# First queries' second layer moved into the second half of a mixture-of-experts loop, with operands made ahead for the last part

## The chip, the cores and the metric

One Trainium2 chip, one core of it. The metric is the device time of one launch in microseconds. The engines named below: PE (TensorE, matrix multiply), ACT (ScalarE), DVE (VectorE), POOL (GpSimd) and SP (SyncE); SP and POOL also issue the transfers (DMA), each from a queue of its own that is worked through in order.

## The reference, cut to what matters

```python
def _A_ref(x, wqkv, wo):                      # S=2048, D=512, H=32, Dh=16
    q, k, v = ...(x @ wqkv)
    phi = lambda t: jnp.where(t > 0, t + 1, jnp.exp(t)) + 1e-6
    pq, pk = phi(q), phi(k)
    kv = einsum("bhsd,bhse->bhde", pk, v)
    z  = einsum("bhsd->bhd", pk)
    o  = (pq . kv) / (pq . z + 1e-6)
    return o @ wo

def _B_ref(x, w_gate, w1, w2):                # E=8, F=1792, K=8: every expert is used
    gates = softmax(x @ w_gate)
    for e in range(E):
        out = out + gates[:, e] * (silu(x @ w1[e]) @ w2[e])

g = sigmoid((x * gate_w).sum(-1))
return g * _A_ref(x, wqkv, wo) + (1 - g) * _B_ref(x, w_gate, w1, w2)
```

All values are float32.

## The kernel before

The output has two addends that share one loop. An expert is two matrix products with `silu` between them. The attention half is put into the same form: its "first layer" is the query projection with `phi` in place of `silu`, its "second layer" is a matrix that the kernel makes from `kv` and `wo` (`wpd`, four tiles written in `fold`). So the loop treats the queries as a ninth expert of smaller width.

Every operand is split into a high and a low part (`act_copy` rounds to the high part on ACT, a `tensor_sub` on DVE gives the low part), and `mm3` (L57 to L60) multiplies in three passes. The block products use seven instead of eight multiplications, in a fixed order of products `ORDER = P1, P7, P2, P4, P6, P5, P3`, with sums and differences of blocks made on DVE (`prep` for weights, `differ` for hidden values).

The tokens are handled in two halves, h = 0 and 1. A *part* is one expert (or the queries, e == E) on one half. An expert's part has 7 *groups* (pairs of 128 hidden features) and 49 *ticks* of second layer; a query part has 2 groups and 14 ticks. The loop runs over steps `u`. Seven steps make the first layer of one group (`up`), each step one product on PE of 6 matmuls of 128x512; the same step does one tick of second layer (`tick`, again 6 matmuls) for an earlier part. The second layer is `LAG` = 58 steps behind. The order of the work on every engine is written out by hand: what `up`, `other` and `mid` emit is the order in each engine's queue.

Groups run in the order: queries of half 0, the eight experts of half 0, queries of half 1, the eight experts of half 1 (`m.groups`, L109 to L113; `m.G1` is where half 1 begins). Second layers run in the order of `m.parts`: eight experts of half 0, eight of half 1, and then both query parts, 28 ticks at the end. Since the queries of half 1 put 14 steps of first layer between the halves, the second half runs at `LAG1` = 72 steps behind, and `clock` (L526) leaves 14 steps at the joint without a tick. After the last group, at step 812, steps hold a tick alone.

What lies around the change:

- `load` (L147) brings the raw weights of a group, from SP. Where `with_second(part)` holds, it also brings the second-layer weights, and `prep` splits those and writes them to DRAM (`stash`, seven transfers of 256 KB for a group, from two buffers of tag `ws`). This holds for the experts of half 0 and for the queries of half 1, whose two groups carry `wpd`.
- `load_w2` (L688) brings one 512 KB tile of stashed second-layer weights for every two ticks, from SP, into three buffers.
- `x_next` (L626) brings the split input blocks of half 1 in steps G1-1 and G1: 14 tiles of 512 KB, from SP.
- `hidden` (L553) applies `silu` on ACT, or `phi` (two passes on ACT, one on DVE) and a store to `pqd`.
- `evict` (L717) and `finish` (L708) take a finished product out of PE's banks: for an expert, a multiplication by its gate (`wb`) on DVE and an accumulating DMA into `acct` from POOL; for the queries, an addition to `sums`, tiles that `load_sums` (L898) has read back.
- `queries_load`, `queries_first`, `queries_last` divide the queries by the normaliser, 20 steps for each of four blocks, in the first four parts of half 1. `load_query` (L891) reads the results back from POOL.
- `rows` (L919) turns `sums` on PE and writes the output.
- `gates` (L811) makes softmax and sigmoid of the gate logits after step 11. `normaliser` and `gate_rows` follow.
- `keys`, before the loop, makes `phi(k)`, the gate logits and `kv`. Its first products wait for the first loads and splits.

Of the kernel before, what the change touches and what calls it, by code (L numbers as in the profile page):

```python
# [42 lines left out]
def gated_mix_kernel(ctx: ExitStack, tc: tile.TileContext, xT, x, wk, wv, wqkv_q, wo, wm, out):  # L43
# [58 lines left out]
    m.parts = [SimpleNamespace(e=e, h=h, n=NPAIR) for h in range(2) for e in range(E)]  # L102
    m.parts += [SimpleNamespace(e=E, h=h, n=2) for h in range(2)]
# [4 lines left out]

    m.groups = []  # L109
    for i in (2 * E, *range(E), 2 * E + 1, *range(E, 2 * E)):  # L110
        part = m.parts[i]
# [3 lines left out]
    m.G1 = m.parts[2 * E + 1].g0  # L115
# [15 lines left out]
def weights(m):  # L131
# [12 lines left out]
    def with_second(part):  # L144
        return (part.e == E) == (part.h == 1)

    def load(g):  # L147
        if g >= m.NG:
            return
        part, q = m.groups[g]  # L150
        both = with_second(part)
        if g >= m.G1 + 4:
# [12 lines left out]
        if both:  # L165
            for i in range(2):
                src = m.wm[part.e * NPAIR + q][:, i, D:] if part.e < E else m.wpd[2 * q + i]
                nc.sync.dma_start(r[:, :, i, 1, :], src.rearrange("p (h f) -> p h f", h=2))
# [4 lines left out]
    def o_tile(name, tag, bufs, width):  # L173
        return w1p.tile([P, 2, width], F32R, name=name, tag=tag, bufs=bufs)

    def prep(g, step):
# [21 lines left out]
        def stash(prod, src):  # L200
            i = part.e * 7 * NPAIR + m.ORDER.index(prod) * part.n + q
            nc.sync.dma_start(m.w2stash[i // 2][:, i % 2].rearrange("p (c f) -> p c f", c=2), f32(src))

# [4 lines left out]
        def low2(n, src, *prods):  # L208
            if both:
                w = ws.pop((g, n))  # L210
                v.tensor_sub(two(w, 1), src, f32(two(w, 0)))  # L211
                for half, prod in enumerate(prods):
                    stash(prod, w[:, :, half * HALF:(half + 1) * HALF])
# [15 lines left out]
        elif step == 2:  # L229
            o = ops[g][6][0]  # L230
            v.tensor_sub(o[:, 1], r[:, 1, 1, 0], f32(o[:, 0]))
            if both:
                w = ws.pop((g, 0))
                v.tensor_sub(w[:, 1, :HALF], r[:, 0, 0, 1], f32(w[:, 0, :HALF]))
                stash("P1", w[:, :, :HALF])
# [19 lines left out]
    m.raw_tile, m.load, m.prep = raw_tile, load, prep  # L255
# [3 lines left out]
def keys(m):  # L259
# [46 lines left out]
    sp = sf_tile("sp")[:NH, :].rearrange("p (c f) -> p c f", c=KT)  # L306
# [22 lines left out]


# [45 lines left out]
    band(sp, [[P, KT], [1, P]], -DH)  # L376
    spread = sf_tile("spread", F32R)
    for i in range(2):
        act_copy(spread[i * NH:(i + 1) * NH], sp.rearrange("p c f -> p (c f)"))
    nc.gpsimd.memset(f32(spread)[2 * NH:], 0.0)  # L380
    nc.gpsimd.dma_start(m.spd, f32(spread))
# [9 lines left out]
    def g_done(t, g, ps):  # L391
        if g == 0:
# [4 lines left out]
            pk[t] = sf_tile(f"pk{t}"), h  # L397
# [50 lines left out]

    banks = [up_bank(f"g0_{t}")[:, :G[0]] for t in range(NTT)]
# [60 lines left out]
def experts(m, misc):  # L510
# [5 lines left out]
    NE = 2 * E  # L516
# [4 lines left out]
    LAG1 = LAG + 14  # L521
    T1 = E * PT
    U1 = LAG + T1
    part_of = [part for part in m.parts for _ in range(7 * part.n)]

    def clock(u):  # L526
        return u - (LAG if u < U1 else LAG1)


    def mine(n, u):  # L530
        return 0 <= n < T1 if u < U1 else T1 <= n < NTICK
# [111 lines left out]

    def differ(u):
# [3 lines left out]
        for pairs, offs in ((NPAIR, (None, 6, 15, 29)), (2, (-3, -1, 1, 5))):  # L648
            for kind, off in enumerate(offs):
                if off is None or not mine(clock(u) - off, u):  # L650
                    continue
                n = clock(u) - off
                part, prod, q = place(n)
                if part.n != pairs or prod != "P1":
                    continue
                t11, t12, t21, t22 = blocks(part, q)
                if kind == 0:
                    v.tensor_sub(t12, t22, t12)
                elif kind == 1:
                    v.tensor_add(t11, t11, t12)  # L660
                elif kind == 2:
                    v.tensor_sub(t21, t21, t11)
                else:
                    v.tensor_sub(t11, t22, t11)
# [3 lines left out]
    def high(n):  # L668
        part, prod, q = place(n)
        s = blocks(part, q)[SRC[prod]]  # L670
        if n % 6 == 5:
            h = m.xpool.tile([P, 2, TB], F32R, name=f"ho{n}", tag="xs", bufs=2)
# [11 lines left out]
    NW = T1 // 2  # L684

    ENDS = (NU + 12 - LAG1) // 2

    def load_w2(i):  # L688
        at, tag, bufs = (m.w1p, "o", 4) if i > ENDS and i % 2 else (m.w2p, "w2", 3)
        w2s[i] = at.tile([P, 2, 2, HALF], F32R, name=f"w2{i}", tag=tag, bufs=bufs)  # L690
        j = i % NW if i < 2 * NW else NW + (i - 2 * NW) % 7
# [10 lines left out]
    def load_wb(i):  # L702
        e, h = m.parts[i].e, m.parts[i].h
        wb[e, h] = m.xpool.tile([P, 2, TB], F32, name=f"wb{i}", tag="xs", bufs=2)
# [12 lines left out]
    def evict(part, prod, sub):  # L717
        b = pb[BANK[prod], sub]
        e = f"{part.h}_{part.e}{sub}"
        if part.e == E:  # L720
# [90 lines left out]
    def gates():  # L811
        g, wgt, gat, mx = m.lg[:, :, :E], m.wgt, m.gat, m.mx
        v.tensor_reduce(mx, g, axis=AX.X, op=ALU.max)
        v.tensor_sub(g, g, mx[:, :, None].to_broadcast([P, NT, E]))
        nc.scalar.activation(wgt, g, AF.Exp)
        nc.scalar.activation(gat, m.lg[:, :, E], AF.Exp, scale=-1.0)
        v.tensor_scalar(gat, gat, 1.0, None, op0=ALU.add)
        v.reciprocal(gat, gat)
        v.tensor_reduce(mx, wgt, axis=AX.X, op=ALU.add)
        v.reciprocal(mx, mx)  # L820
        v.tensor_mul(wgt, wgt, mx[:, :, None].to_broadcast([P, NT, E]))
        v.tensor_scalar(mx, gat, -1.0, 1.0, op0=ALU.mult, op1=ALU.add)
        v.tensor_mul(wgt, wgt, mx[:, :, None].to_broadcast([P, NT, E]))
# [15 lines left out]
    Q = SimpleNamespace(az=None)  # L839

    def queries_load(i):
        if Q.az is None:
            Q.az = m.raw_tile("az", F32R)
# [47 lines left out]
    def load_query(h, i):  # L891
        q, f, t = i // 4, i // 2 % 2, i % 2
        part = m.parts[NE + h]
        d = raw[part.g0 + q, f, t] = r_tile(f"q{h}{i}")
        nc.gpsimd.dma_start(d, m.pqd[h, t, 2 * q + f])


    def load_sums(h, j):  # L898
        for dt in range(KT):
            if dt % 2 == 0:  # L900
                r = m.xpool.tile([P, 2, TB], F32, name=f"tl{h}{j}{dt}", tag="x", bufs=14)
            sums[h, dt, j] = r[:, dt % 2]
            nc.gpsimd.dma_start(r[:, dt % 2], m.acct[h, j, dt])
# [7 lines left out]
    def rows_out(ps, h, i):  # L911
        r = r_tile(f"o{h}{i}")
# [6 lines left out]
    def rows(h, i):  # L919
        ps = ps_tile(f"o{h}{i}", "a")  # L920
        turn(ps, h, i, range(KT), True)
        rows_out(ps, h, i)
# [5 lines left out]
    END = NTICK - 28  # L928
    for u in range(LAG1 + NTICK):
        n = clock(u)  # L930
# [3 lines left out]
        i, s = divmod(n - T1 + 3, PT)  # L934
        s -= 3
        query = u >= U1 and 0 <= i < 4 and s < 20

        def mid():
            if mine(n, u):
                tick(n)  # L940
            if query:
                queries_last(i, s)

        m.spare = ho_tile if u < LAG - 8 else None

        def other():
# [6 lines left out]
            limit = T1 if u < U1 else NTICK  # L953
            while lows < min(n + 4, highs, limit):
# [3 lines left out]
            while highs < min(n + 5, limit):  # L958
                high(highs)
                highs += 1  # L960
            if query:
                if s == -3:
                    queries_load(i)
                queries_first(i, s)

# [9 lines left out]
        if u == 11:  # L975
            gates()
# [7 lines left out]
        if u == 20:  # L984
            load_wb(0)
        if mine(n, u) and n > 7 and n % PT == 3 and n < 2 * T1:
            load_wb(n // PT)
        limit = T1 // 2 if u < U1 else NTICK // 2
        while loaded < limit and loaded <= (n + (5 if u < NU + 8 else 9)) // 2:
# [4 lines left out]
        if g == G1 - 1 and k != 1:  # L994
            x_next(max(k - 1, 0))
        if g == G1 and k == 1:
            x_next(6)
        if u < U1:
            continue
# [6 lines left out]
        if -18 <= at < -2 and at % 2 == 0:  # L1006
            load_query(1, (at + 18) // 2)
        if at in (3, 5):
            load_sums(1, (at - 3) // 2)
        if 11 <= at < 15:  # L1010
            rows(0, at - 11)
        if 16 <= at < 20:
            rows(0, NTT + at - 16)
        if 24 <= at < 28:
            rows(1, at - 24)
# [5 lines left out]
    for tt in range(NTT):  # L1021
        rows_out(last[tt], 1, NTT + tt)
# [39 lines left out]
```

## Time and profile before

| | |
|---|---|
| median of 3 runs | 2379.05 us (2378.55 to 2380.18) |
| profiled execution, its own time | 2379.32 us |
| its span, first to last instruction | 2377.6 us |
| PE, DVE, ACT, POOL busy | 99%, 77%, 59%, 6% |
| granted clock of PE, mean | 0.995 |
| HBM read and written | 344.61 MB, 161.42 MB |

The profiled execution took 2379.32 us, 0.27 us more than the median; 1.7 us of it lie outside the span. "Busy" of PE counts pipelined matmuls that overlap, so a stretch in which PE is 100% busy can still be slow: the number of matmuls in a stretch says more. A timeline row has start, length, engine, line, operation, out<-in, shape and count, and in brackets the idle time before it and what ended it. A row of a stretch has its bounds, its length, and for each engine the busy time and in brackets the number of instructions, then the granted clock of PE (1.00 is full speed), the share of time in which the DMA engines were busy, and GB/s.

### The profile page before, as it was taken

The numbers are of one execution on the slowest core, as the hardware profiler recorded it, in microseconds if no ns is written. First come the engines' busy times: TensorE is split into PE (matmuls) and PEld (weight loads), VectorE is DVE, ScalarE is ACT, GpSimd is POOL, SyncE is SP. The second block draws the span as 40 slices with busy tenths as digits, with TensorE's granted clock in tenths as the row PEclk, the third lists the DMA queues.
The fourth block names the chain that finished last, engine by engine and source line by source line (L and its number), as shares of the span: only waits on it lengthen the run. The fifth ranks groups of instructions, "written<-read, shape, count | busy, mean of one in ns | idle before, by whom it ended". The sixth has DMA issues, their size and how long they took to land. (4 is left out here: it accounts for less than half of the span.)

```text
span 2377.6 us, 31361 instructions
## 1 busy us (share of the span) xinstructions
PE 2344.5 (99%) x10483; PEld 1936.6 (81%) x10483; DVE 1828.4 (77%) x3107; ACT 1409.6 (59%) x2648; POOL 152.8 (6%) x218
## 2 busy tenths in 40 slices
PE   8999999999999999999899999999999999999998
PEld 8877888888888888888688888888888888888876
DVE  6788878888888878888576867777686676766678
ACT  6676666666666666666565555555555555555444
POOL 1110000000000000000000000000000000000121
PEclk9999999999999999999899999999999999999999
DMA  7798888988888898988854444454554454454586
GB/s 217 231 299 286 262 282 253 274 264 269 268 264 281 253 288 252 275 264 270 311 172 145 152 142 165 149 166 151 169 156 145 138 150 140 148 151 132 161 288 234
DMA packets 297041, 512.31 MB, mean 215 GB/s; under 512 B 24224, under 2 KB 193072, under 8 KB 296496
## 3 DMA queue, kind: packets, MB, share of 16 engines
q1 hardware_dynamic: 274048, 463.84, 58.5%
q0 software_dynamic: 22832, 46.49, 10.1%
q8 instruction: 82, 1.34, 0.2%
q14 instruction: 79, 0.65, 0.1%
HBM read 344.61 MB, written 161.42 MB: 213 GB/s over the span
## 5 line engine op out<-in xcount | busy, mean ns | idle before, releaser
L58 PE MATMUL p<-ho,w 128*128 128x512 f32 x1624 | 635.6, 391 | 8.8 <-DMA w<-w2stash 5.8
L59 PE MATMUL p<-ho,w 128*128 128x512 f32 x1624 | 632.9, 390 | 0.0
L60 PE MATMUL p<-ho,w 128*128 128x512 f32 x1624 | 632.8, 390 | 0.0
L680 DVE TENSOR_TENSOR ho<-s,ho 128x512 fp32r<-128x512 f32 x784 | 536.4, 685 | 64.0 <-ACT ho L63 62.3
L63 ACT ACTIVATE ho<-s 128x512 fp32r<-128x512 f32 x784 | 486.6, 621 | 18.2 <-PE p L60 12.6
L58 PEld LDWEIGHTS p<-ho,w 128*128 128x128 f32 x1624 | 305.3, 188 | 78.3 <-ACT p L63 6.8
L60 PEld LDWEIGHTS p<-ho,w 128*128 128x128 f32 x1624 | 305.4, 188 | 63.7
L59 PEld LDWEIGHTS p<-ho,w 128*128 128x128 f32 x1624 | 305.5, 188 | 62.9
L556 ACT ACTIVATE s<-s 128x512 f32<-128x512 f32 x224 | 141.3, 631 | 264.9 <-DVE s L618 198.2
L63 ACT ACTIVATE o<-rm 128x512 fp32r<-128x512 f32 x248 | 141.1, 569 | 83.2 <-PE a L60 59.1
L618 DVE TENSOR_TENSOR s<-c,s 128x512 f32<-128x512 f32 x116 | 80.0, 690 | 136.5 <-PE c L60 132.3
L63 ACT ACTIVATE ws<-rm 128x512 fp32r<-128x512 f32 x214 | 120.7, 571 | 83.5 <-DMA w2stash<-ws 72.9
L63 ACT ACTIVATE o<-rs 128x512 fp32r<-128x512 f32 x216 | 122.7, 568 | 65.4 <-PE a L60 62.7
L624 DVE TENSOR_TENSOR s<-a,s 128x512 f32<-128x512 f32 x116 | 80.0, 690 | 70.5 <-PE a L60 70.2
L556 ACT ACTIVATE s<-b 128x512 f32<-128x512 f32 x112 | 67.1, 599 | 111.8 <-PE b L60 100.2
L193 DVE TENSOR_TENSOR o<-rm,o 128x512 fp32r<-128x512 f32 x186 | 127.3, 685 | 1.8 <-ACT o L63 1.6
L63 ACT ACTIVATE s<-a 128x512 f32<-128x512 f32 x116 | 69.1, 596 | 90.7 <-PE a L60 90.6
L211 DVE TENSOR_TENSOR ws<-rm,ws 128x512 fp32r<-128x512 f32 x162 | 111.0, 685 | 9.0 <-ACT ws L63 9.0
L193 DVE TENSOR_TENSOR o<-rs,o 128x512 fp32r<-128x512 f32 x162 | 110.8, 684 | 9.2 <-ACT o L63 9.0
L63 ACT ACTIVATE s<-c 128x512 f32<-128x512 f32 x116 | 69.0, 595 | 26.0 <-PE c L60 26.0
L63 ACT ACTIVATE b<-a 128x512 f32<-128x512 f32 x116 | 67.1, 578 | 21.1 <-PE a L60 20.7
L714 POOL DMA_DIRECT2D acct<-c x28 | 24.0, 858 | 849.7 <-DVE c L710 612.6
(290 smaller groups left out, 4522.0 us busy)
## 6 DMA issues: line engine op xcount, KB each, us to landing
w<-w2stash SPq DMA_DIRECT2D x406, 512.0 KB, 3.9
w2stash<-ws SPq DMA_DIRECT2D x376, 256.0 KB, 4.3
rm<-wm SPq DMA_DIRECT2D x228, 256.0 KB, 5.3
rs<-wm SPq DMA_DIRECT2D x108, 256.0 KB, 4.0
wb<-wgtd SPq DMA_DIRECT2D x16, 512.0 KB, 5.1
w2stash<-wx SPq DMA_DIRECT2D x30, 256.0 KB, 5.5
acct<-c POOLq DMA_DIRECT2D x28, 256.0 KB, 5.6
acct<-d POOLq DMA_DIRECT2D x28, 256.0 KB, 5.4
```

Source lines behind the costliest of these rows:

```text
L58: nc.tensor.matmul(ps, wh, xh, start=start, stop=False, skip_group_check=True)
L59: nc.tensor.matmul(ps, wh, xl, start=False, stop=False, skip_group_check=True)
L60: nc.tensor.matmul(ps, wlo, xh, start=False, stop=stop, skip_group_check=True)
L63: nc.scalar.activation(dst, src, AF.Copy, scale=scale, bias=bias)
L193: v.tensor_sub(two(o, 1), src, f32(two(o, 0)))
L211: v.tensor_sub(two(w, 1), src, f32(two(w, 0)))
L556: nc.scalar.activation(dst, src, AF.Silu)
L618: v.tensor_add(sn[g, 2], bank[g, "c"], sn[g, 2])
L624: v.tensor_add(sn[g, 3], bank[g, "a"], sn[g, 3])
L680: v.tensor_sub(h[:, 1], s, f32(h[:, 0]))
L714: nc.gpsimd.dma_start(m.acct[part.h, j, dt], s, accum_op=ALU.add)
```

## The change

- Second layers run as: experts of half 0, experts 0 to 3 of half 1, queries of half 0 (A[0]), experts 4 to 7 of half 1, queries of half 1 (A[1]). First layers: A[0], half 0, experts 0 to 3 of half 1, A[1], experts 4 to 7 of half 1. The lag is 58 throughout, and no steps are left without a tick.
- `wpd` is loaded and split by `load_wp` and `prep_wp` in steps 525 to 567 and no longer in the groups of A[1].
- A[0] adds its results to `acct` by accumulating DMA. Its output rows are turned and written in the loop (`rows_first`, eight groups from group 105 on). The last expert adds to `sums` on DVE in place of `acct`.
- For A[1], the last 14 ticks, high and low parts and block differences are made at set ticks from 20 before its start on (`AHEAD`), its weights are loaded into other pools up to 54 ticks ahead, and `sums` are read 42 and 40 ticks ahead.
- `gates` is cut in four, after steps 8, 9, 11 and 12.
- At the start nine matmuls on a zero tile go ahead of the first product; three of four rounding copies of the first weights move from DVE to ACT; the `spread` matrix is made on POOL alone, in another pool, so that the `sf` buffers are left to `pk`.

The diff, cut to its core:

```diff
-    m.parts += [SimpleNamespace(e=E, h=h, n=2) for h in range(2)]
+    X = [[SimpleNamespace(e=e, h=h, n=NPAIR) for e in range(E)] for h in range(2)]
+    A = m.A = [SimpleNamespace(e=E, h=h, n=2) for h in range(2)]
+    M = E // 2
+    m.parts = [*X[0], *X[1][:M], A[0], *X[1][M:], A[1]]
...
-    for i in (2 * E, *range(E), 2 * E + 1, *range(E, 2 * E)):
+    for part in (A[0], *X[0], *X[1][:M], A[1], *X[1][M:]):
...
+    m.beside = [*X[1][:2], *X[1][M:M + 2]]
...
     def with_second(part):
-        return (part.e == E) == (part.h == 1)
+        return part.e < E and part.h == 0
...
+    def load_wp(q):
+        wp[q] = raw_tile(f"wr{q}")[:, :2 * D].rearrange("p (r h f) -> p r h f", r=2, h=2)
+        for i in range(2):
+            nc.sync.dma_start(wp[q][:, :, i], m.wpd[2 * q + i].rearrange("p (r f) -> p r f", r=2))
+    def prep_wp(q, step):
+        ...
...
+    zero = m.w1p.tile([P, 2, D], F32R, name="zero", tag="ws", bufs=2)[:, 0]
+    nc.gpsimd.memset(f32(zero), 0.0)
...
-        split(r0[:, k, :], g0[:, 0, k, :], g0[:, 1, k, :], v.tensor_copy)
+        split(r0[:, k, :], g0[:, 0, k, :], g0[:, 1, k, :], v.tensor_copy if k == 0 else act_copy)
...
+    idle = dn_bank("idle")
+    for i in range(9):
+        nc.tensor.matmul(idle, zero[:, :P], zero, start=True, stop=True)
...
-    LAG1 = LAG + 14
...
     def high(n):
...
+        if END <= n < END + 7:
+            h = m.x_tile(f"ho{n}")
+        elif n >= END + 12 or n < END and n % 6 == 5:
+            h = m.x_tile(f"ho{n}", "xs")
...
     def finish(part, s, src, r, sub, j):
         dt = r * 2 + sub
-        v.tensor_mul(s, src, wb[part.e, part.h][:, j])
-        if part.e == 0:
+        if part.e < E:
+            v.tensor_mul(s, src, wb[part.e, part.h][:, j])
+        elif s is not src:
+            act_copy(s, src)
+        if part is m.parts[-2]:
+            d = sums[1, dt, j]
+            v.tensor_add(d, d, s)
+        elif part.e == 0:
...
+    for i in range(14):
+        at = 2 * i - 20 if i < 7 else i - 8
+        ahead(at + 1, 0, low_h, END + i)
+        ahead(at, 2, high, END + i)
+    for kind, ats in enumerate(((-18, -16), (-15, -13), (-9, -7), (2, 3))):
+        for q, at in enumerate(ats):
+            ahead(at, 1, difference, kind, m.A[1], q)
+    WP = 75
...
+    ROWS0 = 105
-    for u in range(LAG1 + NTICK):
+    for u in range(LAG + NTICK):
...
-        if u == 11:
-            gates()
+        if u in (8, 9, 11, 12):
+            gates((8, 9, 11, 12).index(u))
...
         at = n - END
-        if at in (-40, -32):
-            load_sums(0, (at + 40) // 8)
-        if -36 <= at < -20 and at % 2 == 0:
-            load_query(0, (at + 36) // 2)
...
+        if at in (-54, -52, -50, -48):
+            load_w2((END + at + 54) // 2)
+        if at in (-42, -40):
+            load_sums((at + 42) // 2)
+        if at in (-28, -26, -24):
+            load_w2((END + at + 36) // 2)
+        if 10 <= at < 14:
+            rows(at - 10)
```

More of the change, by code (lines that the diff above doesn't have):

```diff
@@ L174, in o_tile, with stash @@
         return w1p.tile([P, 2, width], F32R, name=name, tag=tag, bufs=bufs)
+    def stash(part, q, prod, src):
+        i = part.e * 7 * NPAIR + m.ORDER.index(prod) * part.n + q
+        nc.sync.dma_start(m.w2stash[i // 2][:, i % 2].rearrange("p (c f) -> p c f", c=2), f32(src))
     def prep(g, step):
@@ L649, in differ @@
             for kind, off in enumerate(offs):
-                if off is None or not mine(clock(u) - off, u):
+                if off is None or not 0 <= u - LAG - off < END:
                     continue
[L652 to L664, printed above, removed]
+                part, prod, q = place(u - LAG - off)
+                if part.n == pairs and prod == "P1":
+                    difference(kind, part, q)
     SRC = {"P1": 0, "P7": 1, "P2": 2, "P4": 2, "P6": 0, "P5": 0, "P3": 3}
@@ L957, in other @@
             differ(u)
-            while highs < min(n + 5, limit):
+            while highs < min(n + 5, END):
                 high(highs)
                 highs += 1
-            if query:
+            for _, do, *what in sorted(AHEAD.get(n, ()), key=lambda step: step[0]):
+                do(*what)
+            for i, s in query:
                 if s == -3:
```

239 lines of the change are left out of this document (146 added, 93 removed).

## The prediction

> **What bounds the kernel now.** I read the page first, then PE by stretches of time, then what PE waited for, and then the timeline of the engines around each wait.
>
> ```profile
> span 2377.6 us, 31361 instructions
> ...
> PE 2344.5 (99%) x10483; PEld 1936.6 (81%) x10483; DVE 1828.4 (77%) x3107; ACT 1409.6 (59%) x2648; POOL 152.8 (6%) x218
> ...
> PEclk9999999999999999999899999999999999999999
> ```
>
> PE bounds it, and one slice of the clock row is not at full speed. What a dense stretch costs, and where PE is not dense, is read from the stretches (length, PE busy, number of matmuls, clock):
>
> ```profile
> core 0: us, PE busy (x), PEclk, DMA share, GB/s
> 5.01:29.52 24.51, 23.43 (x132) 1.00 0.80 286
> 127.60:136.91 9.31, 6.10 (x16) 0.64 0.55 184
> 1155.16:1179.50 24.34, 14.34 (x45) 0.72 0.80 297
> 1400.00:2200.00 800.00, 800.00 (x3530) 1.00 0.49 151
> 2256.60:2322.80 66.20, 63.51 (x272) 1.00 0.85 285
> 2322.80:2372.30 49.50, 47.72 (x233) 1.00 0.64 228
> ```
>
> In the long dense stretch a 128x512 matmul takes 800 / 3530 = 0.2266 us, so a tick of six takes 1.36 us and a step with both layers 2.72 us. Against that price the stretches lose: at 127.60, 9.31 - 16 x 0.2266 = 5.7 us; at 1155.16, 24.34 - 45 x 0.2266 = 14.1 us; at 2256.60, 66.20 - 272 x 0.2266 = 4.6 us. The change leaves PE's matmuls as they are, but for nine on a zero tile, so it can only win back such losses or make new ones. What ended PE's waits:
>
> ```profile
> PE a L58 <- DVE s L624: 6.6, 3, 3.2
> PE p L58 <- DMA w<-w2stash: 5.8, 3, 3.9
> PE g L388 <- DVE g L276: 5.0, 1, 5.0
> PE c L58 <- ACT s L63: 4.8, 2, 3.8
> ```
>
> About 2.5% of the span is at stake in all, and each wait has a place of its own. About 0.2% (4.8 us) is what a measurement here can tell from no change.
>
> **The start.**
>
> ```profile
> 5.01 2.04 PE L388 MATMUL g<-g,x00h 128*128 128x256 f32 x8 [5.01 <-DVE g L276]
> 13.31 0.41 PE L388 MATMUL g<-g,x00h 128*128 128x266 f32 x2
> 29.52 0.40 PE L388 MATMUL g<-g,x10h 128*128 128x256 f32 x2
> 10.00 0.68 DVE L347 TENSOR_TENSOR x01l<-x,x01h 128x512 fp32r<-128x512 f32 x1
> 16.89 0.39 ACT L72 ACTIVATE pk<-g 128x256 f32<-128x256 f32 x1 [1.93 <-DMA spd<-spread]
> 2.81 0.52 POOL L367 MEMSET sp<- 32x512 f32 x1
> ```
>
> The last operand of the first 48 matmuls is ready at 10.68, the next group begins at 13.31. Eight of these 256-column matmuls took 2.04 us, twice half of 0.2266 each: the clock was at half. A memset of 512 columns takes 0.52 us, so nine zero matmuls can run from about 1.5 us, while PE waits anyway, and end near 5.4 us at half clock. With the clock up, the last four matmuls follow at 0.11 us each and the group ends near 11.3: 2.0 us less. From 13.31 to 29.52 are 16.2 us, against 48 matmuls of 266 columns (0.118 by columns) and 36 of 512, 13.8 us: 2.4 us lost. ACT's 1.93 us wait for the spread transfer, which the change removes with its buffer, is in the chain of that. I take 2.0 of the 2.4: together **-4.0** (bounds: -2.0, if the second part stays, and -4.4; 0 if PE is not warm in time). The copies that move to ACT go into ACT's gaps between loads; without these gaps, three copies at 0.39, 1.2 us.
>
> **The gates.**
>
> ```profile
> 118.53 0.69 DVE L74 SCALAR_TENSOR_TENSOR s<-s,a 128x512 f32<-128x512 f32 x1 [1.91 <-ACT a L73]
> 123.83 0.28 DVE L813 TENSOR_REDUCE mx<-lg 128x16 f32<-128x128 f32 x1
> 124.94 0.17 DVE L817 TENSOR_SCALAR gat<-gat 128x16 f32<-128x16 f32 x1 [0.50 <-ACT gat L816]
> 127.21 0.68 DVE L618 TENSOR_TENSOR s<-c,s 128x512 f32<-128x512 f32 x1
> 130.46 0.68 DVE L624 TENSOR_TENSOR s<-a,s 128x512 f32<-128x512 f32 x1
> 131.20 0.79 PE L58 MATMUL a<-t6h,o 128*128 128x512 f32 x1 [3.21 <-DVE s L624]
> 131.79 0.63 PE L59 MATMUL a<-t6l,o 128*128 128x512 f32 x1
> 132.22 0.63 PE L60 MATMUL a<-t6h,o 128*128 128x512 f32 x1
> ```
>
> DVE is without a gap from 118.53 to L618 except for the 0.50 us it waits for ACT. In pieces, its gate work still lies in front of L618, only earlier. What goes is that 0.50 and the two last small operations (about 0.37 with their spacing), which now come behind L618. So L618, L624 and PE come about 0.9 us sooner, and PE's wait is 3.21 - 0.9 = 2.3 us. After the wait the matmuls are 0.43 us apart (131.79 to 132.22): the stretch's clock of 0.64 over 9.31 us is 6.7 us at half speed, worth 3.3 us. Does 2.3 us still bring the clock down? At 1155 the same reckoning gives 24.34 x 0.28 x 2 = 13.6 us at half; 6.7 and 13.6 are about two and four times 3.4, so I estimate that the clock is set in a raster of 3.4 us, by how much of one was idle. If half of it (1.7 us) decides, a wait of 2.3 us falls within one in (3.4 - 2.3) / 3.4 = 32% of positions, and is cut so that one part is still 1.7 us in 2 x 0.6 / 3.4 = 35%: 67%. So I take it that the clock still falls: **-1.5** (0.9, and a somewhat shorter slow stretch; bounds 0 and -5.7).
>
> [...]
>
> **The joint of the halves.**
>
> ```profile
> ACT ws L63 <- DMA w2stash<-ws: 23.4, 5, 8.6
> L202 SPq DMA_DIRECT2D w2stash<-ws x10: 370/371/552, 1131.3 to 1167.0; - x10
> 1125.50:1170.00 44.50, 36.81 (x148) 29.42 (x147) 23.28 (x40) 19.77 (x39) 1.69 (x2) 0.86 1.03 361
> 1145.00:1150.00 5.00, 5.00 (x24) 4.14 (x23) 2.91 (x5) 3.54 (x7) 0.00 (x0) 1.00 1.02 406
> 1179.27 0.50 PE L58 MATMUL a<-n6h,o 128*128 128x512 f32 x1 [2.31 <-DVE s L624]
> ```
>
> Here `x_next` asks for 14 x 512 KB while the queries of half 1 write their stashes. The DMA engines are full (share 1.03); ACT waits 23.4 us for its stashes to leave their two buffers, and PE waits for weights (3.9) and for ACT (3.8). The 44.5 us moved 44.5 x 361 = 16.1 MB. After the change the queries are gone from here and half 1's experts write no stashes: the ten stashes of 256 KB go, and half a megabyte net of loads, about 3.1 MB. That leaves 13.0 MB in the 36 us that the stretch would take unstalled (PE was busy for 36.81), 361 GB/s, and large transfers ran here at 406. So both waits and the slow clock go. The third wait of the stretch (the row at 1179.27, 2.3 us, the queries' `phi` behind a DVE that ACT had held up) moves with the queries to steps 602 to 616, without stashes beside it; I leave 1 us of it. 14.1 - 1.0: **-13.1** (bounds: -6, if the transfers still fill the queue and one wait with its clock stays; -14.1). The covers are the margin of 406 over 361 and the lead of a weight tile, which `load_w2` asks for up to five ticks (13.6 us) ahead.
>
> **The queries' second layer in the loop.** A[0]'s 14 ticks move from the end to steps 646 to 659, where a step has 2.72 us and not 1.36. Its evictions come every two ticks, through four `ot` tiles that are free again when POOL's accumulation has landed. No row shows this beside first layers; the five waits for ACT in the row below (1.5 us for two query parts at half the step) bound it above, with 0 below. The preparation of `wpd` adds 16 operations on DVE in 42 steps, and `rows_first` 8 copies; DVE has room in half 1. POOL's `load_query` stands ahead of accumulations, but by the order of the built program its buffers are released some ten ticks before, so it does not block them. **+0.5**.
>
> **The end.**
>
> ```profile
> PE p L58 <- ACT p L63: 1.5, 5, 0.5
> 2301.33 0.69 DVE L745 TENSOR_TENSOR d<-p,d 128x512 f32<-128x512 f32 x1 [0.90 <-PE p L60]
> 2303.27 0.68 DVE L664 TENSOR_TENSOR s<-s,s 128x512 f32<-128x512 f32 x1
> 2303.87 0.68 DVE L745 TENSOR_TENSOR d<-p,d 128x512 f32<-128x512 f32 x1
> 2304.61 0.50 PE L58 MATMUL p<-ho,w 128*128 128x512 f32 x1 [0.60 <-DVE d L745]
> ```
>
> DVE takes 0.60 us for each operation (2303.27 to 2303.87). Between the two L745 of the last expert, which free PE's banks after P6, stand three operations, and PE already waits 0.60 us for the second. Afterwards there are six: the new addition to `sums`, a low part and a difference made ahead. That is +1.8 us at this bank change; one addition more at P2 to P4 is +0.6; and at P5 to P3 DVE arrives late from the work ahead and has one more between, which I put at +1.7. Against it: A[0]'s waits for ACT leave the end and A[1]'s operands are ready, -2.1 with the slow first matmul after each; fewer POOL loads around 2260, where PE waited for weights, -1.0. Sum **+1.0** (bounds -4, if the operands ahead cover all, and +5, if every bank change waits as the P6 one).
>
> **Sum.** -4.0 - 1.5 - 13.1 + 0.5 + 1.0 = -17.1. From the profiled 2379.3 that is 2362.2; the median lies 0.27 us lower than that run, so 2361.9 us.
>
> **The rivals.**
>
> *The clock stays up at the gates.* The wait of 2.3 us does not suffice; for it: after the wait of 2.31 us at 1179.27 the first matmul took 0.50 us and not 0.79 as at 131.20, so that wait left the clock up. Price -3.3: 2358.6. Chance 0.22. [...]
>
> *The joint still chokes.* `x_next` alone fills the queue, weights come late by one wait of 3.9 us, and the clock falls for 6.7 us (3.3 us): 2361.9 + 7.2 = 2369.1. For it: 361 of 406 GB/s is a thin margin. Against: no stash blocks ACT any more. Chance 0.16.
>
> *DVE becomes the bound at the end: slower.* The built program gives DVE 79 operations in the last 34 ticks, 79 x 0.60 = 47.4 us, and PE 34 x 1.36 = 46.2 us. If the two alternate and do not overlap, more than half of PE's time is idle, the clock stays at half, and a tick takes 6 x 0.43 = 2.58 us: 34 x 1.22 = +41 us, 2403. It decides from where the end loses over 17.1 + 4.8 = 22 us, 18 ticks at half clock. Against: the clock stays at 1.00 through the end now, and the extra operations bunch at two places. Chance 0.04.
>
> *It does not pay:* gains cancel against late DVE and a choked joint together, 2379. Chance 0.04.
>
> **How the numbers follow.** Forecast 0.54, 2361.9. Range 2352 to 2370: the lower end is the clock rival with the end at -4 and the start and joint at their bounds; the upper end takes in the choked joint. Outside are the last two rivals and the tails of the sizes. Faster 0.54 + 0.22 + 0.16 = 0.92, same 0.04, slower 0.04.
>
> **What would show it.** Right: PE near 11.3 us done with the first group; a wait for L624's successor near 2.3 us after the gates; at the joint no wait of PE over 1 us, the clock row at 9 throughout the middle; a DMA share under 1 there; a wait of PE for DVE of about 2.4 us in the last expert. Wrong: the clock row still dropping near 1150 (the margin was misjudged), PE waiting at steps 646 to 659 for `ot` tiles, or the end losing over 10 us to DVE.

## The result and the profile after

The changed kernel takes 2364.62 us (median of 4 runs, 2363.5 to 2365.48), the kernel before 2379.32 us beside it (4 runs, 2378.55 to 2380.18). The ratio is 0.9938, with a 95% interval of 0.9921 to 0.9955: faster, by 0.6%. The forecast was 2361.9 us in a range of 2352 to 2370, so the result lies inside the range and 2.7 us above the forecast.

The profiled execution of the changed kernel took 2363.5 us, 1.1 us less than its median; its account below is against the 2379.32 us of the profiled execution before. From its page (span, granted clock by slice):

```profile
span 2361.7 us, 31380 instructions
...
PEclk9999999999999999999999999999999999999999
```

The 8 in the clock row, at the joint, is gone. The waits of PE, with total, times and longest in us:

```profile
PE p L58 <- ACT p L63: 3.5, 5, 1.4
PE p L58 <- DVE d L809: 2.8, 1, 2.8
PE a L58 <- DVE s L670: 2.4, 2, 2.0
...
PE p L58 <- ACT ho L63: 0.9, 1, 0.9
PE p L58 <- DMA w<-w2stash: 0.7, 1, 0.7
```

The waits for weights (5.8, now 0.7) and for the first operands (5.0, now under the zero matmuls) have shrunk; two waits at the end, for DVE d (2.8) and ACT ho (0.9), are new or longer. The stretches (bounds, length, then busy time and number of instructions of PE, of its weight loads, of DVE, ACT and POOL, then PE's clock, DMA share and GB/s):

```profile
124.68:133.85 9.17, 7.14 (x26) 5.31 (x25) 7.38 (x15) 8.05 (x16) 2.40 (x5) 0.81 0.66 213
1120.00:1165.00 45.00, 45.00 (x199) 36.91 (x198) 29.57 (x53) 24.36 (x46) 1.70 (x2) 1.00 0.92 332
...
2305.00:2355.70 50.70, 44.84 (x199) 35.52 (x200) 38.74 (x61) 15.92 (x27) 0.00 (x0) 0.97 0.08 30
```

At the joint, 45 us hold 199 matmuls, 0.226 us each: dense. Around the place of A[0]'s second layer, 1799 to 1837 us, PE waits for nothing. The last one holds the trouble that is left.

An account by place uses one measure for both kernels: for each matmul, the time to the next one's start less the median of its shape, added up over a stretch. It is the time that PE lost there, idle or at half clock.

| place | before | after | change | forecast |
|---|---|---|---|---|
| start (first matmul of the second block) | 29.52 | 26.60 | -2.9 | -4.0 |
| gates, 110 to 140 us | 8.00 | 6.16 | -1.8 | -1.5 |
| 178 to 200 us | 3.65 | 2.99 | -0.7 | none |
| joint, 1115 to 1215 us | 15.79 | 0.09 | -15.7 | -13.1, with the next row |
| both query parts' new places, 1700 to 1850 us | -0.15 | 0.99 | +1.1 | +0.5 for A[0] |
| 1250 to 1320 us (first block of the queries' division by the normaliser) | 0.83 | -0.04 | -0.9 | none |
| end, from 2245 us | 9.10 | 13.33 | +4.2 | +1.0 |

These sum to -16.7; the pieces between add +0.4, and what follows the last matmul +0.4, which leaves -15.9, against -15.8 between the two profiled executions.

### The profile page after: what moved, and what is told of

Read it like the earlier page. It is cut to its first block, busy times and chain, and to the rows that moved or that the text cites. A ratio compares the mean times of both kernels' runs of the same rounds, so it can differ in the third digit from the quotient of the medians.

```text
span 2361.7 us, 31380 instructions
## 1 busy us (share of the span) xinstructions
PE 2340.9 (99%) x10492; PEld 1935.5 (82%) x10492; DVE 1829.1 (77%) x3112; ACT 1411.2 (60%) x2655; POOL 149.9 (6%) x214
## 4 chain that ended last, share of the span: by engine, by line
PE 93%; DVE 3%; ACT 1%; issue 1%; DMA 1%; SPq 0%; DVEq 0%; ACTq 0%
PE p L58 15%; PE p L60 15%; PE p L59 15%; PE a L58 8%; PE a L60 8%; PE a L59 8%; PE c L60 4%; PE c L59 4%; PE c L58 4%; PE b L60 2%; PE b L59 2%; PE b L58 2%; PE g L438 2%; DVE ho L730 1%; PE y L58 1%
```

## The experiments

The theory was the prediction's own: the stashes at the joint cost what was lost there, the waits for DVE at the gates and at the end come from the order of DVE's work. The rivals for the joint were that the queries' `phi`, or the long lag and the missing ticks, cost the time and not the stashes. Ratios are against the kernel before, run on the same chip beside them (its medians 2380.1, 2379.41 and 2379.51 us). The changed kernel was not run again beside them, so a difference to its 2364.62 us compares runs of different times, between which the kernel before moved by up to 0.8 us; a difference of that size shows nothing by itself.

**1. The stashes back at the joint.** The changed kernel; two groups of half 1 write their second-layer weights to DRAM again, which no one needs.

```diff
-    def with_second(part):
-        return part.e < E and part.h == 0
+    def with_second(part, q):
+        return part.e < E and part.h == 0 or part is X0 and q < 2
```

> The changed kernel, with the second-layer weights of expert 0 loaded, split and stashed a second time in the first two groups of half 1, so that 14 stashes stand beside x_next at the joint again, without the queries. Theory (stashes and x_next together fill the transfers): ACT waits over 15 us for its stashes to leave, PE waits again at the joint by 4 us or more and its clock falls there, 2369 to 2378 us. Rival (the queries' phi and its chain made the joint slow): a loss of no more than 1 us there, 2364 to 2366 us.

Measured: 2382.46 us, ratio 1.0011 [1.0002, 1.002]: all that the change wins is gone, and more. Its waits of ACT and PE between 1115 and 1215 us, and the stretch that stood dense above:

```profile
ACT ws L63 <- DMA w2stash<-ws: 30.4, 7, 13.8
PE c L58 <- ACT s L63: 9.4, 1, 9.4
...
1120.00:1165.00 45.00, 33.33 (x141) 26.65 (x139) 18.17 (x31) 14.08 (x29) 1.70 (x2) 0.86 0.96 347
```

The wait of ACT for its stash buffers, 23.4 us before and absent after, is back at 30.4 us, and PE waits 9.4 us for ACT. The loss from 1115 to 1215 us is 18.3 us, 18.2 more than in the changed kernel, and the medians differ by 17.8. It is more than the theory's upper end of 2378. This kernel stashes all seven products of two ordinary groups, 14 transfers instead of the ten of the queries, and one wait of ACT is 13.8 us where the longest before was 8.6; that the number of stashes makes this difference was not tested.

**2. Only the preparation of `wpd` moved, in the kernel before.** `wpd` is loaded, split and stashed in steps 651 to 693, much as in the changed kernel; queries, lag, start, gates and end stay as they were before.

```diff
-        return (part.e == E) == (part.h == 1)
+        return part.e < E and part.h == 0
...
+            wq, wt = divmod(u - 7 * 93, 21)
+            if 0 <= wq < 2 and wt == 0:
+                m.load_wp(wq)
+            if 0 <= wq < 2 and wt > 2 and wt % 2 and wt < 19:
+                m.prep_wp(wq, (wt - 3) // 2)
```

> The kernel before, in which only the preparation of wpd is taken out of the query groups at the joint and done in steps 651 to 693; the queries of half 1 stay at the joint. Theory (stashes): of the 15.8 us lost between 1130 and 1205 no more than 3 stay, about 2366 us. Rival (the queries' phi): most of it stays, 2375 us or more.

Measured: 2364.53 us, ratio 0.9932 [0.9918, 0.9947]. Its joint:

```profile
1120.00:1165.00 45.00, 45.00 (x200) 37.25 (x199) 29.78 (x52) 24.87 (x45) 2.82 (x4) 1.00 0.97 343
```

The loss there from 1115 to 1215 us is 0.8 us, and PE's longest wait 0.4. So the rivals fall: the queries and the lag of 72 can stay at the joint, the transfers with `x_next` among them run at 343 GB/s without such a wait, and this one edit is worth as much as the whole change. The rest of the change nets nothing: what the start and the gates bring, the end and A[1]'s new place take.

Two things stay open. Both experiments move the loads, the splitting and the stashes together; that it is the stashes among these is read from ACT's rows. And it is not shown how they hurt. The theory says by their volume. But SP issues stashes, `x_next` and weights from one queue in order, and at the joint it also waited for DVE to finish what a stash holds. In the kernel before, between 1115 and 1185 us:

```profile
SPq L202 <- DVE ws L211: 15.9, 5, 5.5
```

While SP waits there, the loads that stand behind the stash wait too: after the wait of 4.1 us that ended at 1166.6, the next weight load was issued at 1167.59. In experiment 1 the same wait (L182 there) is 16.7 us, in the changed kernel 1.9. No run separates the volume from the queue's order.

**3. The gates in one piece**, in the changed kernel.

```diff
-        if u in (8, 9, 11, 12):
-            gates((8, 9, 11, 12).index(u))
+        if u == 11:
+            for step in range(4):
+                gates(step)
```

> The changed kernel with all four pieces of the gates after step 11 again. Theory (the pieces only take 0.9 us from in front of the addition that PE waits for): PE waits 2.9 to 3.2 us and not 2.0, the clock is at half for 3.4 or 6.8 us, 1 to 3 us more than the changed kernel. Rival (the pieces matter by nothing, since DVE is full there): the wait stays at 2.0 us.

Measured: 2365.4 us, ratio 0.9935 [0.9919, 0.9952], 0.8 us over the changed kernel. PE's wait for the tick after the gates is 2.77 us in place of 2.03, and the loss from 110 to 140 us 7.6 in place of 6.2. The wait is a little shorter than the theory's 2.9 to 3.2, but far from the rival's 2.0. The pieces are worth 0.7 us of wait and 1.4 of loss, where the prediction had 0.9 and 1.5; in the total this is within the scatter of the runs, and the ratios to the kernel before (0.9935 and 0.9938) don't show it.

**4. The gates four steps earlier**, in the changed kernel: after steps 4, 5, 6 and 7.

```diff
-        if u in (8, 9, 11, 12):
-            gates((8, 9, 11, 12).index(u))
+        if u in (4, 5, 6, 7):
+            gates(u - 4)
```

> The changed kernel, with the four pieces of the gates after steps 4, 5, 6 and 7 instead of 8, 9, 11 and 12. In the changed kernel's trace PE still waits 2.03 us at the first tick after the gates, the clock then falls for 3.4 us, and the stretch loses 4.0 us in all. Theory: the wait is what the gate work leaves on DVE ahead of the sums of that tick, so four steps earlier it has drained; PE waits 0.5 us or less there, the clock stays up, and the time is 1.5 to 3.5 us under the changed kernel's 2364.6: 2361 to 2363. Rival: the gate work only moves to another place where DVE is as late (the same wait turns up some steps earlier, between 112 and 125 us); time within 0.8 of 2364.6.

Measured: 2362.47 us, ratio 0.9927 [0.9913, 0.9941], 2.2 us under the changed kernel. PE's wait there is 0.46 us and the clock stays up (1.00 from 124.45 to 133.62 us), yet the loss from 110 to 140 us falls by 1.5 only. Behind it stands a wait that was not among PE's larger ones (three rows of ACT and one of PE):

```profile
130.56 1.28 ACT L602 ACT_TABLE_LOAD   x1
...
133.20 0.63 ACT L63 ACTIVATE o<-rm 128x512 fp32r<-128x512 f32 x1 [0.74 <-DVE rm L242]
133.74 0.58 ACT L63 ACTIVATE s<-a 128x512 f32<-128x512 f32 x1
134.37 0.50 PE L58 MATMUL a<-t5h,o 128*128 128x512 f32 x1 [1.69 <-ACT s L63]
```

ACT goes over from `phi` to `silu` here, which takes it a table load of 1.28 us; the copy that frees PE's bank then stands behind a weight copy that itself waits 0.74 us for DVE. PE waits 1.69 us. Which of the two, the load or the wait for DVE, makes it late was not tested.

**5. No matmuls on the zero tile**, in the changed kernel: the nine and their memset are left out.

```diff
-    idle = dn_bank("idle")
-    for i in range(9):
-        nc.tensor.matmul(idle, zero[:, :P], zero, start=True, stop=True)
```

> The changed kernel without the nine matmuls on zeros. Theory: the first 48 matmuls run at half clock until about 10.7 us and end near 13.3 and not 12.25, and since the rest of the start's gain comes from the spread buffers, the step to the second block of tokens is reached about 1 us later than in the changed kernel, 2365.7 us. Rival (the whole gain of 2.9 us at the start is the warm clock): 2.9 us later.

Measured: 2364.77 us, ratio 0.9932 [0.9917, 0.9947]. The second block begins at 27.81 us in place of 26.60, and the first group ends at 13.46 in place of 12.25, so the nine matmuls are worth 1.2 us at the start: near the theory's 1, far from the rival's 2.9. The total (0.15 us more) can't show that, since runs of one kernel spread over 1 to 4 us. This run shows something else. The wait after the gates is 2.03 us again, as in the changed kernel, but the clock does not fall. Stretches of 3.41 us, first of the changed kernel, then of this one:

```profile
124.69:128.10 3.41, 1.38 (x6) 0.86 (x5) 2.61 (x6) 2.46 (x5) 0.54 (x1) 1.00 0.27 100
128.10:131.52 3.41, 3.41 (x10) 2.57 (x9) 2.50 (x4) 3.41 (x9) 0.54 (x1) 0.50 0.83 283
```

```profile
123.65:127.07 3.42, 2.65 (x16) 1.99 (x14) 2.43 (x7) 1.99 (x4) 0.00 (x0) 1.00 0.68 256
127.07:130.48 3.41, 2.15 (x10) 1.77 (x11) 2.76 (x7) 2.46 (x5) 0.54 (x1) 1.00 0.59 205
130.48:133.90 3.42, 3.42 (x16) 2.79 (x15) 2.79 (x6) 3.40 (x10) 0.68 (x2) 1.00 0.82 276
```

In the changed kernel the wait lies in one such stretch, PE is busy for 1.38 us of it, and the next has clock 0.50. Here the wait is cut in two by the line at 127.07 us, PE is busy for 2.65 and 2.15 us, and the clock stays at 1.00. Even so, the loss from 110 to 140 us is 6.20 us, as much as the 6.16 with the clock down, because the wait of experiment 4 now shows (1.68 us at 137.38).

**6 to 8. The end.** (6) The last expert's additions to `sums` wait in a list and run some ticks later; (7) A[1]'s operands and differences are made earlier, and its queries read back earlier for that; (8) both.

```diff
-            d = sums[1, dt, j]
-            v.tensor_add(d, d, s)
+            LATER.append((sums[1, dt, j], s))
...
+            if n - END in (-27, -26, -12, -11, -5, -4):
+                d, s = LATER.pop(0)
+                v.tensor_add(d, d, s)
...
+        if at in (-2, -1):
+            d, s = LATER.pop(0)
+            v.tensor_add(d, d, s)
```

```diff
-        at = 2 * i - 20 if i < 7 else i - 8
+        at = (-26, -25, -24, -23, -14, -13, -11)[i] if i < 7 else i - 8
...
-    for kind, ats in enumerate(((-18, -16), (-15, -13), (-9, -7), (2, 3))):
+    for kind, ats in enumerate(((-25, -24), (-23, -22), (-12, -11), (2, 3))):
...
-        for part, at in ((m.A[0], -18), (m.A[1], -36)):
-            i, odd = divmod(n - part.t0 - at, 2)
+        for part, at, by in ((m.A[0], -18, 2), (m.A[1], -38, 1)):
+            i, odd = divmod(n - part.t0 - at, by)
```

> The changed kernel with the last expert's eight additions to sums put off by some ticks, out from between the operations that free PE's banks. Theory (DVE's queue holds PE at the bank changes): PE's wait after P6 falls from 2.8 to about 1.6 us, its clock stays up there, the waits after P2 and P5 shrink by 0.5 each, 2 to 3 us less than the changed kernel, about 2362 us. Rival (PE waits for operands that ACT makes late): the waits stay, 2364.6 us.

> The changed kernel with the operands of the last query part made 6 to 8 ticks earlier, where DVE has one operation a tick, or between bank changes, and none at the bank changes themselves. Theory (DVE's queue): the wait after P6 falls from 2.8 to about 1.6 us, the 0.9 us wait for ACT just ahead of it goes, the clock stays up, about 3.5 us less than the changed kernel, 2361 us. Rival (the work only shifts and comes back at another bank change): within 1 us of 2364.6.

> Both of the two last edits. Theory: PE waits under 1 us at each bank change of the last expert, the end loses about 5 us less than in the changed kernel, 2359.5 us. Rival (DVE is the bound there by its sum of 79 operations): no better than the better of the two alone.

Measured: 2362.08 us (ratio 0.9928 [0.9913, 0.9942]), 2362.64 us (0.9929 [0.9915, 0.9944]) and 2359.86 us (0.9918 [0.9903, 0.9933]): 2.5, 2.0 and 4.8 us under the changed kernel. The runs of (7) spread from 2360.34 to 2364.79 us, so its total alone shows little; the losses from 2245 us on, 11.4, 11.0 and 9.1 us in place of 13.3, show that both edits gain and that the gains add. PE's wait at the bank change after P6 was 2.8 us in the changed kernel (its row stands with the waits above). In these three, in order, it is:

```profile
PE p L58 <- DVE d L809: 2.1, 1, 2.1
```

```profile
PE p L58 <- DVE d L809: 1.3, 1, 1.3
```

```profile
PE p L58 <- DVE d L809: 0.7, 1, 0.7
```

The theory had 1.6 us for (6) and for (7); in (6) the wait is longer, and the clock still fell behind it, to 0.50. With both edits the wait is 0.7 us, near the 0.6 us of the kernel before, the clock stays at full speed there (1.00 from 2303 to 2312 us), and the loss at the end is 9.08 us, that of the kernel before (9.10). So the places of these operations on DVE are worth as much as the end's +4.2 us, and the rival that the sum of DVE's operations is the bound falls. The theory's "under 1 us at each bank change" did not hold: one wait for DVE, further on (L812), is 1.4 us.

**9. The spread matrix made after the first weights are split**, in the changed kernel.

```diff
-    spread = m.w1p.tile([P, 2, D], F32, name="spread", tag="ws", bufs=2)[:, 0]
-    ...
+    def make_spread():
+        ...
+        if t == 0:
+            make_spread()
```

> The changed kernel with the spread matrix made after the first key tile and not at the very start. In the changed kernel the first DVE operations took 0.79, 1.12 and 0.88 us while POOL was busy, and the same shapes took 0.42 and 0.69 later. Theory (POOL's work slows DVE): these three fall to 0.42 to 0.69 us, and the first group of matmuls ends about 0.5 us sooner; the time is within 1 us of the changed kernel. Rival (the first operations are slow by themselves, or by the loads): they stay.

Measured: 2364.1 us, ratio 0.9939 [0.9923, 0.9956], 0.5 us under the changed kernel, within its spread. Locally the effect is plain. DVE and POOL in the changed kernel, and DVE in this one:

```profile
4.63 0.79 DVE L325 TENSOR_TENSOR g<-r,g 128x256 fp32r<-128x256 f32 x1
5.35 1.12 DVE L398 TENSOR_TENSOR x00l<-x,x00h 128x512 fp32r<-128x512 f32 x1
...
4.52 0.63 POOL L419 TENSOR_SCALAR_AFFINE_SELECT spread<-spread 32x512 f32<-32x512 f32 x1
5.21 0.70 POOL L421 TENSOR_SCALAR_AFFINE_SELECT spread<-spread 32x512 f32<-32x512 f32 x1
```

```profile
4.59 0.42 DVE L325 TENSOR_TENSOR g<-r,g 128x256 fp32r<-128x256 f32 x1
4.93 0.69 DVE L398 TENSOR_TENSOR x00l<-x,x00h 128x512 fp32r<-128x512 f32 x1
7.22 0.42 DVE L325 TENSOR_TENSOR g<-r,g 128x256 fp32r<-128x256 f32 x1 [1.60 <-ACT g L63]
```

Without POOL beside them the same operations take 0.42 and 0.69 us in place of 0.79 and 1.12. Little is won by it, 0.4 us at the second block (26.20 in place of 26.60): the third row now waits 1.60 us for a copy on ACT, and in the changed kernel that copy, at 6.81 us, had waited 1.10 us for the transfer of its weights.

**10. All of it together**: the gates four steps earlier, both edits at the end, and the spread matrix later; its edits are the diffs of experiments 4 and 6 to 9, unchanged.

> All edits that the runs so far found useful, in one: the changed kernel with the gates' pieces four steps earlier, the last expert's additions to sums put off, the operands of the last part made some steps earlier, and the spread matrix made on POOL only after the first weights are split. Theory: the places lie apart, so the gains add: -4.8 at the end (measured for the two edits there together), -1.5 to -3.5 at the gates, and -0.5 for the spread: 2356 to 2358. Rival: the gates' edit wins nothing and the end is all there is: 2359.3 to 2360.

Measured: 2357.45 us (5 runs, 2357.23 to 2358.06), ratio 0.9905 [0.9891, 0.992]: 7.2 us under the changed kernel. The gains of the parts (4.8, 2.2 and 0.5 us) sum to 7.5. Its longest waits of PE:

```profile
PE p L58 <- ACT p L63: 2.6, 4, 1.4
PE a L58 <- ACT s L63: 2.4, 2, 1.7
...
```

No wait is over 1.7 us, and the profiled execution's mean granted clock is 1.000, against 0.998 in the changed kernel. The end still loses 9.4 us, about what the kernel before lost there.

## Why the prediction was right or wrong

The sign and most of the size came from one term, the joint, and that term was right in its place and its remedy: experiment 1 puts the stashes back and the loss returns, experiment 2 takes the preparation of `wpd` away alone and the gain is there. That the transfers were too many for the time is argued; the order in SP's queue is left as a rival. Of the step's two covers, the margin of the transfers held: they ran at 332 GB/s in the dense stretch, and no wait for weights stayed at the joint. The 1 us that was left for the queries' `phi` in its new place is there (0.6 us of wait at 1722 us, 1.0 lost). The rival that the joint still chokes falls with that.

That the sum came out only 2.7 us off is in part luck. The end lost 3.2 us more than forecast and the start won 1.1 less; against that, the joint with the rows at 1700 to 1850 us won 2.0 more, and 1.6 us came from places that were not forecast.

**The start** was taken at -4.0 and gave -2.9. The second part had the right size: from the second group to the second block are 26.60 - 12.25 = 14.35 us in place of 16.2, 1.9 of the assumed 2.0. ACT's wait for the spread transfer is gone from that stretch; that the whole 1.9 is its worth is not shown, as no run puts that wait back alone. Nor is 29.52 a fixed mark: in experiment 2, whose start is that of the kernel before, the clock fell in this stretch, and the second block began at 31.55. The first part was too large: the group ended at 12.25 and not at 11.3.

```profile
9.38 1.11 PE L438 MATMUL g<-g,x01h 128*128 128x256 f32 x8
...
12.25 0.41 PE L438 MATMUL g<-g,x00h 128*128 128x266 f32 x2
...
6.81 0.42 ACT L63 ACTIVATE g<-r 128x256 fp32r<-128x256 f32 x1 [1.10 <-DMA r<-wk]
```

The step that failed is "the last four matmuls follow at 0.11 us each" after the last operand. The clock was up from 5.22 us, as forecast (the nine zero matmuls ahead of it took 4.07 us, 0.45 each, against 0.226 in the dense stretch), and the last operand was ready at 10.62, as before; but by then PE was further behind. From 9.38 on it runs without a wait, 24 matmuls at 0.12 us, and these set the end. The group's 48 matmuls from 5.36 on take 5.8 us at that price, up to 11.1, and another 1.1 us went in short waits for earlier operands. Bounding the group by its last operand left these out. One cause of the late operands is POOL beside DVE (experiment 9, 0.4 us). Another is the transfer of the weights, for which ACT's copy at 6.81 had waited 1.10 us; in the kernel before, DVE's copy of the same weights waited for it until 6.57.

**The gates** were taken at -1.5 and gave -1.8; the wait was 2.03 us for a forecast of 2.3, and the clock fell, for one stretch of 3.41 us instead of two. The raster that the prediction estimated from two numbers is there: both half-clock stretches of the changed kernel before its last matmul last 3.41 us. Its guess that 1.7 us of idle time in a stretch decides is not far from what that trace shows: 2.03 and 2.58 us without work (1.38 and 0.83 busy) were followed by half clock, 1.65 (1.76 busy) was not. What was wrong is the price of the rival. The prediction gave the clock's staying up 3.3 us. It is worth nothing here: the loss from 110 to 140 us is 6.2 us in each of seven kernels with the wait of 2.03 us, four with the clock down (6.16 to 6.28) and three with it up (6.20 to 6.22). The wait behind it takes up the difference: from the matmul after the first wait to the one after the second are 9.05 to 9.15 us in all seven, with the second wait 1.7 us long when the clock is up and 0.2 or less when it is down. By the rows of experiment 4 that second wait is for ACT's work around the table load.

**A[0] in the loop** at +0.5 was too cautious: no wait, and no more than 0.2 us lost.

**The end** is the term that was mis-sized: +1.0 forecast, +4.2 measured.

```profile
2304.24 0.68 DVE L809 TENSOR_TENSOR d<-p,d 128x512 f32<-128x512 f32 x1
2304.95 0.69 DVE L769 TENSOR_TENSOR d<-d,wb 128x512 f32<-128x512 f32 x1
2305.68 0.69 DVE L774 TENSOR_TENSOR tl<-tl,d 128x512 f32<-128x512 f32 x1
2306.29 0.69 DVE L730 TENSOR_TENSOR ho<-s,ho 128x512 fp32r<-128x512 f32 x1
2306.89 0.69 DVE L699 TENSOR_TENSOR s<-s,s 128x512 f32<-128x512 f32 x1
2307.49 0.69 DVE L730 TENSOR_TENSOR ho<-q,ho 128x512 fp32r<-128x512 f32 x1
2308.09 0.68 DVE L695 TENSOR_TENSOR q<-q,q 128x512 f32<-128x512 f32 x1
2308.70 0.68 DVE L809 TENSOR_TENSOR d<-p,d 128x512 f32<-128x512 f32 x1
2309.44 0.80 PE L58 MATMUL p<-ho,w 128*128 128x512 f32 x1 [2.80 <-DVE d L809]
2310.88 0.63 PE L58 MATMUL p<-ho,w 128*128 128x512 f32 x1
2311.31 0.63 PE L59 MATMUL p<-ho,w 128*128 128x512 f32 x1
```

Between the two L809 stand six operations, as forecast, and the wait is 2.80 us for a forecast of 2.4 (0.60 + 1.8). Three things went wrong around it. The tick before it waits 0.9 us for `ho`, again behind DVE, which no step had priced. Behind the wait another 1.6 us are lost, which no step had priced either: here as half clock (0.43 us between seven matmuls), which the prediction had reckoned with at the gates and not here. The clock is not the whole cause, though. In experiments 1, 3 and 4 the same wait of 2.8 us is there and the clock stays up; they lose 10.13 to 10.15 us from the matmul at 2303 us on to the end, and the changed kernel and experiments 5 and 9, with the clock down, 10.23 to 10.37. Where the clock stays up, a second wait of 0.9 us for `ho` follows instead. So DVE's order costs this much either way, and the slow stretch itself about 0.1 to 0.2 us.

The third thing is that the 2.1 us that operands made ahead were to win on waits for ACT did not come: the last part still loses 2.5 us to them, against 2.4 for both parts before. Their rows name `p`, PE's banks, and not `ho`; ACT copies the finished products out of the banks, and operands made ahead don't change that. In the longest one ACT's copy stands behind another operand copy that waits for DVE:

```profile
2336.96 0.63 ACT L63 ACTIVATE ho<-q 128x512 fp32r<-128x512 f32 x1 [1.35 <-DVE q L699]
...
2338.11 0.58 ACT L63 ACTIVATE p<-p 128x512 f32<-128x512 f32 x1
2338.74 0.50 PE L58 MATMUL p<-ho,w 128*128 128x512 f32 x1 [1.43 <-ACT p L63]
```

The other terms were nearer: P2 to P4 +0.7 for +0.6 (there PE waits for ACT, not for DVE), P5 to P3 +0.7 for +1.7, weights -1.2 for -1.0; about -1.0 lies in pieces of 0.2 us and less. The rival that DVE becomes the bound at the end is half right: DVE holds PE, but at single bank changes and not throughout, and its price of 41 us rested on the clock's staying down: it was down for 3.4 us.

Two gains were not forecast, -0.7 between 178 and 200 us and -0.9 between 1250 and 1320 us. No experiment was made on them, and their cause is open. The first is there in experiment 2 too (3.0 us lost, for 3.65), whose edit begins at step 651, so it need not come from the change at all. The second is not (0.9 us lost, for 0.83); there the first sums of the queries' normaliser on PE waited for ACT and DVE, and the changed kernel makes them 40 us earlier, at 1260 us.

## What to carry to other kernels

Where a bulk transfer has a fixed place, move other writers out of that place first: here that one edit was worth the whole change, and it could have been tried alone. When operations are added to an engine that frees another's buffers, count what stands between two frees and set the additions where nothing is released. Before a wait, or the slow clock behind it, is priced as won, look for the wait that ends just behind it: at the gates and at the end that one took the gain. Read from the released name whether operands or buffers are short.

## What the runs showed of the hardware

**The clock changed at lines 3.41 us apart.** In the traces of the two kernels the granted clock changed, up to the last matmul, only at the lines of such a grid. In the kernel before it came up at 10.66 us (256-column matmuls 0.23 us apart from 5.01 on, 0.12 from 11.87 on) and was at half from 130.13 to 136.96 and from 1157.54 to 1171.19, two and four stretches; in the changed kernel it came up at 5.22 and was at half from 128.10 to 131.52 and from 2309.21 to 2312.62, one stretch each. PE's busy time in a full-clock stretch of these two traces, and the clock in the next: 0.83, 1.27, 1.38 and 1.42 us were followed by half clock, 1.76 us and more by full clock. The row with 1.38 stands with experiment 5. In the experiments, 1.35 us was followed by half clock, at the end of experiment 6, and 1.63 and 1.55 were not, at the end of experiment 1:

```profile
2306.62:2310.03 3.41, 1.35 (x6) 1.02 (x6) 3.38 (x7) 0.63 (x1) 0.00 (x0) 1.00 0.00 0
2310.03:2313.45 3.42, 3.42 (x10) 2.65 (x9) 3.42 (x7) 1.69 (x4) 0.00 (x0) 0.50 0.44 152
```

```profile
2323.25:2326.66 3.41, 1.63 (x6) 1.05 (x6) 3.34 (x7) 0.82 (x2) 0.00 (x0) 1.00 0.38 154
2326.66:2330.08 3.42, 1.55 (x7) 1.31 (x8) 3.35 (x7) 0.63 (x1) 0.00 (x0) 1.00 0.00 0
2330.08:2333.49 3.41, 3.41 (x17) 2.83 (x16) 3.41 (x7) 2.25 (x5) 0.00 (x0) 1.00 0.46 154
```

Experiment 1 has the same wait of 2.78 us at that place as the changed kernel's 2.80, but the line at 2326.66 us cuts it, and the clock stayed at 1.00; in the changed kernel all but 0.2 us of it lies in one stretch, and the next had 0.50. So it was with the 2.03 us after the gates, cut by a line in experiment 5 and within one stretch in the changed kernel. One stretch with more work than those of experiment 1 was followed by half clock even so, at the start of experiment 2:

```profile
19.47:22.88 3.41, 1.65 (x6) 1.17 (x7) 2.51 (x6) 2.17 (x7) 0.56 (x1) 1.00 0.53 211
22.88:26.29 3.41, 3.41 (x10) 2.42 (x9) 2.23 (x5) 2.71 (x7) 0.91 (x1) 0.50 0.42 76
```

So stretches with 1.55 to 1.65 us of work were followed by full clock in two places and by half clock in one, and PE's busy time, which counts modelled ends of matmuls, does not tell these apart.

**DVE was slower beside POOL.** While POOL worked on `spread` (its rows stand with experiment 9), DVE's subtractions took 0.79 and 1.12 us; in experiment 9, with no POOL operation there, they took 0.42 and 0.69. DVE's next `x00l` in the changed kernel, at 8.07 us, took 0.68 us, POOL's last operation on `spread` having ended at 7.87. Why POOL's work slows DVE is not shown.
